# Eight 512-wide products of zeros among the transposes of the first query units

## The chip, the cores and the metric

The kernel runs on one core of one Trainium2 chip. The metric is the time of one execution on the device, in microseconds (us). Engines are named as in the profile: PE (TensorE, matrix products and transposes), PEld (its weight loads), DVE (VectorE), ACT (ScalarE), POOL (GpSimd), SP (SyncE, which issues most DMAs).

## What is computed

Agent attention, followed by a mixture of experts with one expert per token. There are 4 batches of 11456 tokens, 128 channels, 49 agents, 8 experts with 1024 hidden units. Cut to what matters:

```python
def sm(a, b):                                   # softmax of scaled scores
    s = scale * (a @ b.transpose(0, 2, 1))
    e = np.exp(s - s.max(-1, keepdims=True))
    return e / (e.sum(-1, keepdims=True) + 1e-09)
agent_v = sm(agents, k) @ v                     # per batch: 49 x 128
x = (sm(q, agents) @ agent_v).reshape(B * N, D)
logits = normed(x) @ normed(expert_emb).T / tau
idx, gate = argmax(logits), softmax(logits)[idx]
out[idx == e] = gate * (relu(x[idx == e] @ w1[e]) @ w2[e])
```

## The kernel before

A batch is cut into 12 units of up to 8 columns of 128 tokens. For each batch the keys come first (their scores against the agents, then the weighted sum of the values, `avp`), then the queries, then the feed-forward part with the one expert that nearly all tokens of the batch pick; the few other tokens are answered one by one. In batches 1 to 3 the keys of the next batch run beside the feed-forward part of the one before. Batch 0 has nothing to run beside, so its keys and the start of its queries stand alone, in `first()`.

The place of the change is the turn of batch 0 from keys to queries. When the values are summed, `av_chain` makes `avT` and the router's columns (`foldp`, `key`, `rp`), and the generator `pick_expert` starts: it has the expert's weights fetched (w1s, w2s, on SP's queue), multiplies them with `avT` (L606, tile `gp`), ranks the hidden units by a key (L645 spreads the key over a diagonal, L656 multiplies it with ones into `row`, L663 and L665 count on DVE and ACT how many are smaller), and sorts the units into place (`sel`, `placed`, then `gh` and `gl`). The first feed-forward product is `hp` (L1040, L1041). `linp` (L708), `w2pp` (L722) and `yp` come after it.

Meanwhile `q_unit` handles the queries. Units 0 and 1 of batch 0 are started first, units 2 and 3 after the first two have been turned; these four (LEAD is 4) run in a special form (`f32` is true). Each unit of 8 columns goes through these steps:

- `pe_T` turns the 8 columns with 8 fp32 transposes on PE into two PSUM banks (tile `fTp`, four columns a bank, from the pool of four banks `ps_h`). ACT copies the first bank out (L395), DVE the second (L393).
- Eight products with the agents give the scores (L773, `sp`). Each shows as two records in the profile.
- DVE takes the maximum and subtracts it (L777, L780), ACT takes the exponential (L782) and rounds it (L787), DVE makes the rest (L788).
- For the four first units, PE turns the result in f16 (L793, `tp`) and ACT copies it out (L794, `tt`). Other units use a DMA for this.
- 16 products with `r_hi` and `r_lo` (L809, L810, `rtp`) give the router's numbers.

`zeros` is a 128 x 512 f16 tile of zeros in SBUF. The kernel already multiplies it with itself 14 times at its start (`warm`, L170), in PSUM banks that nothing reads.

The order of instructions on each engine comes from a scheduler that works on priorities and on a simulated time line of its own: an instruction that is put in may move others. SP's order is fixed by hand (`manual_schedule`).

Of the kernel before, what the change touches and what calls it, by code (L numbers as in the profile page):

```python
# [18 lines left out]
P = 128  # L19
# [10 lines left out]
def kernel(ctx: ExitStack, tc: tile.TileContext, q, k, v, agents, emb, tau, w1, w2, out):  # L30
    nc = tc.nc
    pe, dve, act, pool, sp = nc.tensor, nc.vector, nc.scalar, nc.gpsimd, nc.sync
# [25 lines left out]
    GRP = 2  # L58
    LEAD = min(4, NU)
    LAG = 5  # L60
    HOLD = 2
    TB = 8
    XB = 3
# [20 lines left out]
    def pss(name):  # L84
        return ps_s.tile([P, 512], F32, name=name, tag="s")

    def psh(name):
        return ps_h.tile([P, 512], F32, name=name, tag="h")
# [11 lines left out]
    def take(o, uses=1):  # L100
        at = o.asked
        o.asked += 1
        while len(o.left) < at or (at >= o.n and o.left[at - o.n]):
            yield 1
        o.left.append(uses)
        return at

    def give(o, i):
        o.left[i] -= 1
# [8 lines left out]
    units, slot = {}, {}  # L118

    def used(*unit):  # L120

        ring[slot[unit]][1] = now[0]
# [9 lines left out]
    def unit_of(t):  # L132
        return (t // UT, t % UT) if t < NT - 1 else (NU - 1, 0)

    def ushape(u):
        return (P, min(UJ, J - u * UJ)) if u < NU - 1 else (REM_P, REM_J)

    def ucol(u):
        return min(u * UJ, J)
# [23 lines left out]
    zeros = cst.tile([P, 512], F16, name="zeros")  # L163
# [196 lines left out]
    def in_place(last):  # L360

        return tc.issue_after(last[-1].ins) if last else nullcontext()
# [17 lines left out]
        else:  # L380
            dve.tensor_tensor(out=mr, in0=spv, in1=mr, op=ALU.max)

    def pe_T(src, p, n):

        xT = wk.tile([P, 2 * UJ, P], F16, name="fT", tag="xT", bufs=XB).rearrange("k c p -> k (c p)").bitcast(F32)
        for c0 in range(0, n, TJ):
            m = min(TJ, n - c0)
            tp = psh("fTp")
            for c in range(m):
                pe.transpose(out=tp[:, c * p : (c + 1) * p], in_=src[:p, c0 + c, :], identity=ident[:p, :p])  # L390
            dst = xT[:, c0 * p : (c0 + m) * p]
            if c0:
                dve.tensor_copy(dst, tp[:, : m * p])  # L393
            else:
                act.copy(dst, tp[:, : m * p])  # L395
        return xT
# [362 lines left out]
    def q_unit(b, u, g):  # L759
        bt = batches[b]  # L760
        p, n = ushape(u)
        while ("q", b, u) not in units:
            yield 1
        tt_of[b, u] = yield from take(t_slots, n + sum(unit_of(t)[0] == u for t in range(NT)))
        f32 = b == 0 and u < LEAD
        i = yield from take(x_slots)
        with in_place(p_last):
            xT = pe_T(units["q", b, u], p, n)
        used("q", b, u)
        yield g[0]  # L770
        s = pss("sp")
        for c in range(n):
            pe.matmul(out=s[:p, c * A : (c + 1) * A], lhsT=xT[:, c * p : (c + 1) * p], rhs=aT_all[:, b, :], start=True, stop=True)  # L773
        give(x_slots, i)
        spv = s[:p, : n * A].rearrange("p (c a) -> p c a", a=A)
        mx = sm.tile([P, UJ], F32, name="qmx", tag="qmx")[:p, :n]
        dve.tensor_reduce(out=mx, in_=spv, axis=AX.X, op=ALU.max)  # L777
        ie = yield from take(qe_slots)
        e = wk.tile([P, UJ, A], F32, name="qe", tag="qe", bufs=LEAD)[:p, :n]
        dve.tensor_tensor(out=e, in0=spv, in1=mx.unsqueeze(2).broadcast_to([p, n, A]), op=ALU.subtract)  # L780
        yield g[1]
        act.activation(e, e, AF.Exp, scale=SCALE)  # L782
        yield g[2]
        i = yield from take(e_slots)
        e2 = e16[i % len(e16)]
        hi = e2[:p, :n, :A]
        act.copy(hi, e)  # L787
        (dve if f32 else pool).tensor_tensor(out=e2[:p, :n, LO : LO + A], in0=e, in1=hi, op=ALU.subtract)  # L788
        tt = wk.tile([P, UJ * P], F16, name="tt", tag="tt", bufs=TB)
        if f32:  # L790
            tp = psh("tp").bitcast(F16)
            for c in range(n):
                pe.transpose(out=tp[:, c * p : (c + 1) * p], in_=e2[:p, c, :], identity=ident16[:p, :p])  # L793
            act.copy(tt[:, : n * p], tp[:, : n * p])  # L794
        else:
            if ffn_at[0]:
                yield 4
            sp.dma_start_transpose(out=tt[:, : n * p].rearrange("k (c p) -> k c p", p=p),
                                   in_=e2[:p, :n, :].rearrange("p c k -> p (c k)"))
        give(e_slots, i)  # L800
        yield g[3]
        tts[b, u] = tt
        while not hasattr(bt, "r_hi"):
            yield 1
        s = (pss if ffn_at[0] else psh)("rtp")
        with in_place(y_last):
            for c in range(n):
                o = s[:p, c * RW : (c + 1) * RW]
                pe.matmul(out=o, lhsT=tt[:, c * p : (c + 1) * p], rhs=bt.r_hi, start=True, stop=False)  # L809
                pe.matmul(out=o, lhsT=tt[:, c * p : (c + 1) * p], rhs=bt.r_lo, start=False, stop=True)  # L810
        gi = group_of[u]
        us = groups[gi]
        if (b, gi) not in rtgs:
            rtgs[b, gi] = wk.tile([P, GC, E + 1], F32, name="rtg", tag="rtg", bufs=4)
        if not hasattr(bt, "qq"):
            bt.qq = sm.tile([P, 2, NCOL], F32, name="qq", tag="qq")
        rtg, qq = rtgs[b, gi], bt.qq
        c0 = ucol(u) - ucol(us[0])
        cs = slice(c0, c0 + n)
        if p < P:  # L820
            pool.memset(rtg[p:, cs], 1.0)
            pool.memset(qq[p:, :, ucol(u) : ucol(u) + n], 1.0)
        sv = s[:p, : n * RW].rearrange("p (c w) -> p c w", w=RW)
        rt = wk.tile([P, 2, UJ, A], F32, name="rt", tag="rt", bufs=1)[:p, :, :n]
        act.copy(rtg[:p, cs], sv[:, :, : E + 1])
        pool.tensor_tensor(out=rt[:, 1], in0=e, in1=e, op=ALU.mult)
        dve.tensor_tensor(out=rt[:, 0], in0=sv[:, :, E + 1 :], in1=e, op=ALU.mult)  # L827
        give(qe_slots, ie)
        yield 1
        pool.tensor_tensor(out=rt[:, :, :, : A // 2], in0=rt[:, :, :, : A // 2], in1=rt[:, :, :, A // 2 + 1 :], op=ALU.add)  # L830
        yield g[4]
        dve.tensor_reduce(out=qq[:p, :, ucol(u) : ucol(u) + n], in_=rt[:, :, :, : A // 2 + 1], axis=AX.X, op=ALU.add)
        routed[b, gi] = routed.get((b, gi), 0) + 1
        if routed[b, gi] == len(us):
            spawn(route_group(b, gi, sum(ushape(x)[1] for x in us)), 1, half=True)
# [74 lines left out]
    def proved(b, u, c):  # L910

        bt = batches[b]
        p, n = ushape(u)
        FV = FVS[b]
        at = slice(ucol(u) + c, ucol(u) + c + 1)
        z = psh("vp")
        with in_place(y_last):
            pe.matmul(out=z[:p, :FV], lhsT=tts[b, u][:, c * p : (c + 1) * p], rhs=bt.vm, start=True, stop=True)  # L918
        give(t_slots, tt_of[b, u])
        if c not in (0, 2, 4):  # L920
            act.activation(z[:p, :FV], z[:p, :FV], AF.Relu, bias=bt.l[:p, at], scale=-1.0, accum_out=bt.vsum[:p, at])  # L921
        else:
            dve.tensor_reduce(out=bt.vmin[:p, at], in_=z[:p, :FV], axis=AX.X, op=ALU.min)  # L923
        bt.seen += 1
# [3 lines left out]
    def prove():  # L928

        if jobs and ((jobs[0][0], HOLD) <= ffn_t[0] or jobs[0][0] == 0):  # L930
            proved(*jobs.pop(0))
# [355 lines left out]
    def spawn(g, at=0, half=False):  # L1287
        t0 = now[0] + (now[0] % 2)
        active.append([t0 + 2 * at, g, 1 if half else 2])
# [22 lines left out]
    def first():  # L1312
# [29 lines left out]
        for u in range(2):  # L1342
            spawn(q_unit(0, u, (1, 0, 0, 1, 0)))
# [6 lines left out]
        for u in range(2, LEAD):  # L1350
            spawn(q_unit(0, u, (1, 0, 0, 1, 0)))
# [67 lines left out]
    def queries():  # L1419
        start = now[0] // 2  # L1420
        for at, _, b, u in plan()[1]:
            while now[0] // 2 < start + at + 2:
                yield 1
            spawn(q_unit(b, u, (2, 1, 1, 5, 1)))
# [19 lines left out]
    with tc.manual_schedule(engines={mybir.EngineType.SP}):  # L1444
        due = []
        for i in range(len(ticks) + LAG):
            if i < len(ticks):
                b, t, r = ticks[i]
# [5 lines left out]
                if f is not None:  # L1454
                    with tc.high_priority(200):
                        ffn_mm1(b, t, f)
                    ffn_t[0] = (b, t)
                    due.append((i + LAG, b, t, f))
            else:
                run_half()  # L1460
            while due and due[0][0] <= i:
                _, b, t, f = due.pop(0)
# [49 lines left out]
```

## Time and profile before

| what | value |
|---|---|
| median of 3 runs | 800.28 us (799.91 to 804.07) |
| the profiled execution | 803.49 us |
| its span, first to last instruction | 801.7 us |
| mean granted clock of PE | 0.938 |
| PE busy | 729.7 us (91%) |
| PE weight loads | 614.5 us (77%) |
| DVE busy | 620.7 us (77%) |
| ACT busy | 487.2 us (61%) |
| POOL busy | 347.4 us (43%) |

A span is the time from the first to the last instruction of the profiled execution; its own time is 1.8 us longer. The granted clock is the share of its full clock at which PE was let run. Busy PE is not PE at its peak: its records overlap, and at half clock the same product takes twice as long.

### The profile page before, as it was taken

The numbers are of one execution on the slowest core, as the hardware profiler recorded it, in microseconds if no ns is written. First come the engines' busy times: TensorE is split into PE (matmuls) and PEld (weight loads), VectorE is DVE, ScalarE is ACT, GpSimd is POOL, SyncE is SP. The second block draws the span as 40 slices with busy tenths as digits, with TensorE's granted clock in tenths as the row PEclk, the third lists the DMA queues.
The fourth block names the chain that finished last, engine by engine and source line by source line (L and its number), as shares of the span: only waits on it lengthen the run. The fifth ranks groups of instructions, "written<-read, shape, count | busy, mean of one in ns | idle before, by whom it ended". The sixth has DMA issues, their size and how long they took to land.

```text
span 801.7 us, 21160 instructions
## 1 busy us (share of the span) xinstructions
PE 729.7 (91%) x8161; PEld 614.5 (77%) x8161; DVE 620.7 (77%) x1639; ACT 487.2 (61%) x1229; POOL 347.4 (43%) x602
## 2 busy tenths in 40 slices
PE   8979889989897979979999799999998898999995
PEld 6978678877786768768888588778886687877774
DVE  5554698887674999957678898966779987699876
ACT  2333475877664763657667944766579354666763
POOL 5000341445513743745433742685537445255520
PEclk9985589999997989989999999999999998999998
DMA  8766008997746946965596627986352235122311
GB/s 324 207 203 228 27 1 231 276 236 184 183 132 154 301 86 182 206 180 135 149 283 150 170 72 176 274 203 170 94 142 73 85 97 167 54 73 75 101 54 47
DMA packets 164050, 124.01 MB, mean 155 GB/s; under 512 B 84968, under 2 KB 140348, under 8 KB 163948
## 3 DMA queue, kind: packets, MB, share of 16 engines
q1 hardware_dynamic: 150571, 99.02, 47.5%
q10 hardware_dynamic: 13120, 23.47, 8.1%
q8 instruction: 65, 1.06, 0.5%
q14 instruction: 38, 0.30, 0.1%
q0 software_dynamic: 256, 0.15, 0.1%
HBM read 79.14 MB, written 23.72 MB: 128 GB/s over the span
## 4 chain that ended last, share of the span: by engine, by line
PE 58%; DVE 24%; DMA 8%; ACT 5%; issue 3%; POOL 1%; SPq 0%; ACTq 0%; POOLq 0%; DVEq 0%
PE sp L773 7%; PE fTp L390 6%; PE avp L487 5%; PE sp L411 5%; PE vp L918 4%; PE yp L1068 4%; PE yp L1070 4%; PE yp L1069 4%; PE hp L1040 3%; DVE hl L1045 3%; PE hp L1041 3%; PE yp L1059 3%; DMA tt<-e 3%; DMA kt<-in_k_dram 2%; DVE vmin L923 2%
## 5 line engine op out<-in xcount | busy, mean ns | idle before, releaser
L1045 DVE SCALAR_TENSOR_TENSOR hl<-hp,hh 128x512 f16<-128x512 f32 (+1 forms) x207 | 137.1, 666 | 31.8 <-ACT hh L1044 31.1
L1068 PE MATMUL yp<-w2p,hh 128*128 128x128 f16 (+1 forms) x810 | 157.9, 223 | 1.1 <-ACT hh L1044 0.6
L1069 PE MATMUL yp<-w2p,hh 128*128 128x128 f16 (+1 forms) x810 | 157.7, 222 | 0.0
L1070 PE MATMUL yp<-w2p,hl 128*128 128x128 f16 (+1 forms) x810 | 154.0, 222 | 3.4 <-DVE hl L1045 3.4
L921 ACT ACTIVATE vp<-vp,la 128x320 f32<-128x320 f32 (+1 forms) x224 | 121.7, 543 | 54.3 <-PE vp L918 42.1
L1044 ACT ACTIVATE hh<-hp 128x512 f16<-128x512 f32 (+1 forms) x207 | 120.6, 587 | 46.9 <-PE hp L1041 42.6
L918 PE MATMUL vp<-vm,tt 128*128 128x320 f16 (+1 forms) x360 | 109.5, 323 | 9.9 <-DVE hl L1045 4.3
L1068 PEld LDWEIGHTS <-hh 128*128 128x128 f16 (+1 forms) x810 | 81.8, 101 | 21.2 <-ACT hh L1044 5.1
L773 PEld LDWEIGHTS sp<-aT_all,fT 128*128 128x128 f32 x720 | 94.8, 207 | 3.1 <-DVE rt L827 0.3
L1070 PEld LDWEIGHTS <-hl 128*128 128x128 f16 (+1 forms) x810 | 81.2, 100 | 20.0 <-issue 6.6
L773 PE MATMUL sp<-aT_all,fT 128*128 128x49 f32 x720 | 96.1, 286 | 0.1
L1069 PEld LDWEIGHTS <-hh 128*128 128x128 f16 (+1 forms) x810 | 81.2, 100 | 8.0 <-issue 1.0
L923 DVE TENSOR_REDUCE vmin<-vp 128x1 f32<-128x320 f32 (+3 forms) x136 | 72.2, 531 | 17.6 <-PE vp L918 17.4
L1040 PE MATMUL hp<-tt,gh 128*128 128x512 f16 (+1 forms) x207 | 78.0, 380 | 6.6 <-ACT fT L395 2.1
L1041 PE MATMUL hp<-tt,gl 128*128 128x512 f16 (+1 forms) x207 | 78.0, 380 | 0.0
L788 POOL TENSOR_TENSOR e<-qe,e 128x392 f16<-128x392 f32 (+1 forms) x44 | 38.7, 880 | 81.6 <-ACT e L787 78.0
L869 POOL TENSOR_TENSOR nrm<-qq,half 128x16 f32<-128x16 f32 (+2 forms) x28 | 68.8, 2456 | 0.2
L395 ACT COPY fT<-fTp 128x512 f32<-128x512 f32 (+1 forms) x78 | 43.7, 563 | 38.6 <-PE fTp L390 29.9
L1083 DVE TENSOR_TENSOR ot<-yp,gs 128x512 f32<-128x512 f32 (+1 forms) x92 | 61.3, 668 | 7.4 <-PE yp L1070 7.2
L1059 PE MATMUL yp<-lin,tt 128*128 128x128 f16 x720 | 65.1, 221 | 1.7 <-DVE ot L1083 1.5
L390 PE MATMUL fTp<-ident,qt 128*128 128x128 f32 x360 | 60.6, 303 | 4.5 <-ACT vp L921 1.3
L393 DVE COPY fT<-fTp 128x512 f32<-128x512 f32 x70 | 47.8, 683 | 21.6 <-PE fTp L390 20.4
(358 smaller groups left out, 1750.4 us busy)
## 6 DMA issues: line engine op xcount, KB each, us to landing
kt<-in_k_dram SPq DMA_DIRECT2D x44, 512.0 KB, 6.4
vt<-in_v_dram SPq DMA_DIRECT2D x44, 512.0 KB, 5.3
qt<-in_q_dram SPq DMA_DIRECT2D x44, 512.0 KB, 5.1
out_dram<-ot ACTq DMA_DIRECT2D x88, 256.0 KB, 2.8
w1s<-in_moe_w_dram SPq DMA_DIRECT2D x8, 512.0 KB, 3.7
w2s<-in_moe_w_dram SPq DMA_DIRECT2D x8, 512.0 KB, 5.5
tt<-e SPq DMA_TRANSPOSE x44, 3.2
kt<-in_k_dram SPq DMA_DIRECT2D x4, 96.0 KB, 3.0
```

The costliest lines, as they stand in the source:

```text
L390: pe.transpose(out=tp[:, c * p : (c + 1) * p], in_=src[:p, c0 + c, :], identity=ident[:p, :p])
L773: pe.matmul(out=s[:p, c * A : (c + 1) * A], lhsT=xT[:, c * p : (c + 1) * p], rhs=aT_all[:, b, :], start=True, stop=True)
L918: pe.matmul(out=z[:p, :FV], lhsT=tts[b, u][:, c * p : (c + 1) * p], rhs=bt.vm, start=True, stop=True)
L921: act.activation(z[:p, :FV], z[:p, :FV], AF.Relu, bias=bt.l[:p, at], scale=-1.0, accum_out=bt.vsum[:p, at])
L1040: pe.matmul(out=hp[:, :m], lhsT=bt.gh[:, fs], rhs=tt, start=True, stop=False)
L1041: pe.matmul(out=hp[:, :m], lhsT=bt.gl[:, fs], rhs=tt, start=False, stop=True)
L1044: h_last[:] = [act.activation(hh[:, :m], hp[:, :m], AF.Relu)]
L1045: dve.scalar_tensor_tensor(out=hl[:, :m], in0=hp[:, :m], scalar=0.0, in1=hh[:, :m], op0=ALU.max, op1=ALU.subtract)
L1059: pe.matmul(out=yp[:p, c, :], lhsT=tc_, rhs=bt.lin[:, h], start=(c == 0 and h == 0), stop=False, skip_group_check=True)
L1068: pe.matmul(out=y, lhsT=hh[:, cs], rhs=wh, start=False, stop=False, skip_group_check=True)
L1069: pe.matmul(out=y, lhsT=hh[:, cs], rhs=wl, start=False, stop=False, skip_group_check=True)
L1070: y_last[:] = [pe.matmul(out=y, lhsT=hl[:, cs], rhs=wh, start=False, stop=last, skip_group_check=True)]
```

## The change

`pe_T` takes a number of fillers, and `q_unit` passes 1 for the four first units of batch 0 and 0 for all others. Each filler is one product of `zeros` with itself, 512 columns wide in f16, written into the bank that the next four transposes write. The transposes overwrite it, and nothing reads it. Two banks a unit and four units make eight fillers. The keys' calls of `pe_T` keep 0.

```diff
+    FILL = 1
...
-    def pe_T(src, p, n):
+    def pe_T(src, p, n, fill=0):
...
             tp = psh("fTp")
+            for _ in range(fill):
+                pe.matmul(out=tp, lhsT=zeros[:, :P], rhs=zeros, start=True, stop=True)
             for c in range(m):
                 pe.transpose(out=tp[:, c * p : (c + 1) * p], in_=src[:p, c0 + c, :], identity=ident[:p, :p])
...
-            xT = pe_T(units["q", b, u], p, n)
+            xT = pe_T(units["q", b, u], p, n, FILL if f32 else 0)
```

The lines of the changed kernel are one higher from L59 on, and three higher behind the loop of fillers (L390 becomes L393, L773 becomes L776).

PE, units 0 and 1, from the router's products to the products with the expert's weights. Before (tile names as in the steps above; qt are the loaded queries):

```order
L534 MATMUL rp<-avT 128x49
L390 MATMUL fTp<-ident,qt 128x128 x16
L238 MATMUL total<-avsq,ones 128x1
L773 MATMUL sp<-aT_all,fT 128x49 x12
L553 MATMUL avsT<-ident,avT 49x128
L773 MATMUL sp<-aT_all,fT 128x49 x4
L198 MATMUL mT<-ident,amx 1x128
L203 MATMUL mB<-ident,mTx 128x1
L606 MATMUL gp<-avT,w1s 128x49 x8
```

And now:

```order
L391 MATMUL fTp<-zeros 128x512
L393 MATMUL fTp<-ident,qt 128x128 x4
L391 LDWEIGHTS zeros
L391 MATMUL fTp<-zeros 128x512
L393 MATMUL fTp<-ident,qt 128x128 x4
L239 MATMUL total<-avsq,ones 128x1
L776 MATMUL sp<-aT_all,fT 128x49 x13
L556 MATMUL avsT<-ident,avT 49x128
L776 MATMUL sp<-aT_all,fT 128x49 x3
L199 MATMUL mT<-ident,amx 1x128
L204 MATMUL mB<-ident,mTx 128x1
L609 MATMUL gp<-avT,w1s 128x49 x8
```

Each four transposes have a filler ahead of them (the first two groups stand right ahead of these rows in the same form); the rest keeps its place but for one product of sp.

PE, units 2 and 3, behind the router's products of units 0 and 1. Before:

```order
L390 MATMUL fTp<-ident,qt 128x128 x12
L773 MATMUL sp<-aT_all,fT 128x49 x4
L390 MATMUL fTp<-ident,qt 128x128 x4
L773 MATMUL sp<-aT_all,fT 128x49 x12
L656 MATMUL row<-sel,ones 128x512 x2
```

And now, from the second of four groups on:

```order
L391 LDWEIGHTS zeros
L391 MATMUL fTp<-zeros 128x512
L393 MATMUL fTp<-ident,qt 128x128 x4
L391 LDWEIGHTS zeros
L391 MATMUL fTp<-zeros 128x512
L393 MATMUL fTp<-ident,qt 128x128 x4
L391 LDWEIGHTS zeros
L391 MATMUL fTp<-zeros 128x512
L393 MATMUL fTp<-ident,qt 128x128 x4
L776 MATMUL sp<-aT_all,fT 128x49 x16
L659 MATMUL row<-sel,ones 128x512 x2
```

All sixteen transposes now stand ahead of all sixteen products of sp.

ACT, behind the copies of row, where the rank is counted (sel,more) and the turned scores of units 2 and 3 are copied out (tt) and their router's numbers (rtg). Before:

```order
L665 ACTIVATE sel,more<-sel,nkey 128x1024
L787 CAST e_1_160<-qe 128x8x49
L883 ACTIVATE ex<-lga 128x64
L665 ACTIVATE sel,more<-sel,nkey 128x1024
L794 COPY tt<-tp 128x1024
L665 ACTIVATE sel,more<-sel,nkey 128x1024
L794 COPY tt<-tp 128x1024
L395 COPY fT<-fTp 128x512
L665 ACTIVATE sel,more<-sel,nkey 128x1024
L825 COPY rtg<-rtp 128x72 x2
L683 CAST gh<-placed 128x256
```

And now:

```order
L668 ACTIVATE sel,more<-sel,nkey 128x1024
L790 CAST e_1_160<-qe 128x8x49
L797 COPY tt<-tp 128x1024
L668 ACTIVATE sel,more<-sel,nkey 128x1024
L828 COPY rtg<-rtp 128x72
L668 ACTIVATE sel,more<-sel,nkey 128x1024
L797 COPY tt<-tp 128x1024
L668 ACTIVATE sel,more<-sel,nkey 128x1024
L398 COPY fT<-fTp 128x512
L828 COPY rtg<-rtp 128x72
L686 CAST gh<-placed 128x256
```

The copy of the second unit's scores comes two counts behind the first one's, where one count stood between them; PE's transposes tp and products rtp of these two units are taken apart in the same way. SP issues the same list in the same order as before. Further on, the instructions of PE, DVE, ACT and POOL are the same ones, in an order that differs at several hundred places.

## The prediction

> **What bounds the kernel now.** I read the page's slices first, then the chain of work that ended last in the stretch of the change, then busy time with the granted clock by stretches, and last single groups on PE.
>
> ```profile
> PE   8979889989897979979999799999998898999995
> PEclk9985589999997989989999999999999998999998
> ```
>
> A slice is 20 us. PE is 80% busy or more nearly everywhere, and the granted clock is full except in one long hole, slices 4 and 5 (60 to 100 us). There batch 0 turns from its keys to its queries: units 0 and 1, then 2 and 3, are turned (fTp), scored (sp), and the expert's columns are ranked (gp, row, sel).
>
> ```profile
> 62.26 3.44 PE fTp L390 x16
> 65.91 5.20 PE sp L773 x24
> ...
> 71.32 1.59 PE sp L773 x8
> ...
> 74.39 3.58 PE gp L606 x16
> ...
> 82.98 2.71 PE fTp L390 x12
> 85.68 1.57 PE sp L773 x8
> 87.26 0.88 PE fTp L390 x4
> 88.14 4.99 PE sp L773 x24
> 93.12 3.56 PE row L656 x4
> 96.71 0.58 ACT sel L657
> ...
> 104.39 1.15 ACT sel L665 x2
> ...
> 112.78 0.38 PE hp L1040
> 113.38 0.82 PE sp L411 x8
> ```
>
> These are start, length and work of the chain: up to 96.7 us the path is nearly all PE, and from there to the second feed-forward tile (hp, 112.78) it is mostly ACT and DVE. So a faster PE pays ahead of 96.7 and hardly between 96.7 and 112.8.
>
> ```profile
> 60.42:104.80 44.38, 39.19 (x232) 35.27 (x233) 26.26 (x76) 21.50 (x43) 8.64 (x16) 0.50 0.31 112
> 67.25:70.66 3.41, 3.41 (x18) 3.41 (x18) 1.40 (x3) 1.45 (x3) 0.00 (x0) 0.50 1.11 356
> 84.32:87.73 3.41, 3.41 (x18) 3.19 (x18) 2.96 (x10) 0.78 (x2) 2.67 (x7) 0.50 0.50 148
> 91.14:94.56 3.42, 3.42 (x12) 2.58 (x12) 1.40 (x3) 0.00 (x0) 0.00 (x0) 0.50 0.01 2
> 101.38:104.80 3.42, 3.42 (x43) 3.36 (x42) 3.11 (x8) 3.42 (x6) 0.14 (x1) 0.50 0.00 0
> ```
>
> Columns: stretch, length, busy us of PE, weight loads, DVE, ACT, POOL, then the clock. The clock is 0.50 for 44.38 us although PE is busy for 39.19 of them, and it comes back at 104.80. 44.38 is 13 times 3.41, so I cut the time into stretches of 3.41 us from 60.42. Busy time doesn't bring the clock back: three of the four short rows are 100% busy and the clock stays. What they differ in is how much of it *streams columns*. A transpose takes 3.44/16 = 0.215 us for 128 columns (1.68 ns a column). An sp record takes 5.20/24 = 0.217 us for 49 columns, worth 0.082 us: 38%, the rest is its weight load. So 67.25 to 70.66 (sp alone) streams 38%; 84.32 to 87.73 (about 9 transposes, 8 sp) streams (1.94 + 0.66)/3.41 = 76%; 91.14 to 94.56 (8 sp, then row from 93.1) some 65%. The stretch after which it rose held this:
>
> ```profile
> 101.66 1.91 PE L390 MATMUL fTp<-ident,qt 128*128 128x128 f32 x8
> 103.36 0.26 PE L809 MATMUL rtp<-r_hi,tt 128*128 128x58 f16 x1
> ...
> 104.84 0.19 PE L810 MATMUL rtp<-r_lo,tt 128*128 128x58 f16 x1
> ```
>
> Eight transposes and 32 rtp products (first and last shown) fill it from edge to edge with streaming, some 99%. A later rise, at 258.4 us, followed this stretch:
>
> ```profile
> L390 PE MATMUL fTp<-ident,qt 128*128 128x128 f32 x6 | 1.6, 409 | 0.1
> L1040 PE MATMUL hp<-tt,gh 128*128 128x512 f16 x2 | 1.3, 634 | 0.0
> L1041 PE MATMUL hp<-tt,gl 128*128 128x512 f16 x2 | 1.2, 623 | 0.0
> ```
>
> Six transposes and four 512-wide f16 products: (6 x 0.215 + 4 x 0.427)/3.41 = 88% (0.427 is worked out below). So the point lies between 76% and 88% of a stretch, and a mix of transposes and 512-wide products, just what the change makes, passes it.
>
> **The change part by part.** It adds 8 products of zeros on PE, one ahead of each four transposes in units 0 to 3 of batch 0, and removes nothing.
>
> ```profile
> 1.48 2.31 PE L170 MATMUL warm<-zeros 128*128 128x512 f16 x5 [1.48 <-POOL zeros L164]
> 5.17 1.03 PE L170 MATMUL warm<-zeros 128*128 128x512 f16 x2
> 113.00 0.38 PE L1041 MATMUL hp<-tt,gl 128*128 128x512 f16 x1
> ```
>
> *Price of a filler.* The same product, with the clock not yet up: (2.31 - 1.03)/3 = 0.427 us each. At full clock 512 columns take about 113.00 - 112.78 = 0.22 us, from hp to hp. The weight load stands beside the product ahead. Each unit's fillers write a bank that its transposes take anyway, so no new wait for a bank arises; DMA and SP issue the same list in the same order.
>
> *Units 0 and 1.* Four fillers at 0.427 = +1.7 us on the path. They stretch 3.44 us of transposes to 5.15 us of pure streaming, from 62.3 to 67.4. However the 3.41 us grid lies, one stretch holds 2.6 us or more of it plus sp or rp beside it: 83% at worst. With the grid of this execution 63.83 to 67.25 is full and the clock rises at 67.25. Then sp: 5.20 + 1.59 = 6.79 us becomes 32 x 0.103 = 3.3 (0.103 from the row at 113.38, 0.82/8): -3.5. Its cover is gone with it: next is gp, which needs the weights w1s.
>
> ```profile
> 69.05 1.06 ACT L607 ACTIVATE sel<-w1s 128x1024 f16<-128x1024 f32 x1 [1.47 <-DMA w1s<-in_moe_w_dram]
> 88.78 1.21 DVE L645 TENSOR_TENSOR sel<-ident,key 128x1024 f32<-128x1024 f32 x1
> ```
>
> They are there at 69.05, ahead of gp's new start at 72.6 (74.39 - 1.8), so no wait appears. Does gp gain too? If the clock holds, 3.58 becomes 16 x 0.103 = 1.65 and the small products around it lose 0.4: another -2.3. A clock that was lost again shows the limit:
>
> ```profile
> L918 PE MATMUL vp<-vm,tt 128*128 128x512 f16 x2 | 0.8, 392 | 0.0
> L1040 PE MATMUL hp<-tt,gh 128*128 128x512 f16 x1 | 0.4, 379 | 0.0
> L1041 PE MATMUL hp<-tt,gl 128*128 128x512 f16 x1 | 0.4, 379 | 0.0
> L1121 PE MATMUL sqT<-ident,xq 128*128 128x128 f32 x1 | 0.3, 301 | 2.5 <-DMA xq<-in_q_dram,ix 2.5
> ```
>
> This is the stretch 671.40 to 674.82, after which it fell: four 512-wide and a few narrow products, at full clock's 0.22 us per 512 columns some 1.06 us of 3.41, 31%. The stretch with gp has 38% at most while gp runs, and gaps around mT and mB; I take it that the clock falls, gain 0. Units 0 and 1: +1.7 - 3.5 = -1.8 (bounds +1.7 if nothing rises, -4.1 if it holds).
>
> *Units 2 and 3.* Again four fillers, +1.7, and 5.15 us of streaming right behind rtp. The order also puts all 16 sp products behind all 16 transposes, where 4 of them stood in between; the same work, but one unbroken block. The clock rises in it or at its end. Then sp 1.57 + 4.99 = 6.56 becomes 3.3 (-3.3) and row 3.56 becomes 1.8 (-1.8). Next late is DVE's diag, ended at 89.99 and row at 93.12: 3.1 us of slack, of which 1.7 - 3.3 takes 1.6, so it doesn't bind. Sum -3.4 (bounds: +1.7, and -5.5 where transposes run fast too and DVE binds).
>
> *Behind 96.7.* ACT and DVE set the pace and carry the shift on at its length. The moved order splits tp and rtp of units 2 and 3 (second rtp half behind two more of ACT's sel passes), so the 99% stretch that ended the hole is broken up, and the clock may come later than before, relative to hp. Nearest rows: sp and placed there; each stretch at half clock costs 1.7 us at most, all under ACT or DVE to 0. I take 0, between 0 and 5 (three stretches). From hp on, the stages run in their own order with all engines above half busy, so an earlier start should reach the end. There the same instructions stand in another order at several hundred places on all engines but SP; I find no sign for it, and give it plus or minus 3 us.
>
> *The sum.* -1.8 - 3.4 = -5.2 on a traced execution that took 803.49 us (span 801.7): 798.3. But the median of the runs shown is 800.28 (799.91 to 804.07), 3.2 below it. I read part of that as the grid lying elsewhere: where a stretch falls within 0.4 us of the 3.44 us of transposes (0.8 of 3.41 positions, a quarter) or on rtp and the transposes at 82 us, the kernel before rises by itself, and the change gains only 1.5 or so. With 0.7 and 0.3, an estimate, 0.7 x 5.2 + 0.3 x 1.5 = 4.1, and 800.28 - 4.1 = **796.2 us**.
>
> [...]
>
> **The rivals.**
> (a) *The fillers don't lift the clock*, since transposes count for little. Then fillers stream 1.7 of 5.15 us, 33%, below all that rose; 8 x 0.427 = 3.4 us stay on the path: 803.7. Against it: the two rises above. 6 in 100.
> (b) *Slower: the end of the hole moves out.* The broken 99% stretch leaves the clock at half from row through placed, hp, the key transposes and linp. It decides from 2.4 stretches on (4.1/1.7) in which PE alone is the path; four to six of them make 800.28 - 4.1 + 6.8 = 803 to 806.4. For it: in the old order that one stretch alone passed. Against it: placed and hp are 256 and 512 wide and stream fully. 12 in 100.
> (c) *Half of it is lost*: only one pair of units lifts the clock in time, or the shift is eaten in the moved order behind 112.8: 797 to 802. 30 in 100.
> (d) *The clock holds through gp and row*: -4.1 - 5.5 = -9.6 at most, 790 to 792. 10 in 100.
>
> **How the numbers follow.** My forecast has 42 in 100, with its own range 793 to 798. I take 0.5% (4 us) as what a measurement tells from none: faster is below 796.3. From the forecast a good 35 and from (d) 10, with little of (c), make 0.47 faster; (a), most of (c) and the rest of the forecast 0.39 the same; (b) and a bad draw of the moved order 0.14 slower. The range leaves out the ends of (b) and the best of (d): 790.5 to 803.
>
> **What would show it.** Granted clock 1.00 from about 67 us for one stretch, again from about 82 to 86; sp records 0.10 us apart there; row at 1.8 us; gp still at 0.22 a record; the second hp some 5 us earlier than 112.78; the same shift at the end. It is wrong if the clock stays 0.50 through both blocks, if row comes earlier and hp doesn't, or if hp comes earlier and the end doesn't.

## The result, and the profile after

The changed kernel takes 805.51 us (median of 20 runs, 798.07 to 815.10), the kernel before, run beside it, 800.24 us (20 runs, 792.62 to 807.61). The ratio is 1.0083, 95% interval 1.0054 to 1.0113: slower by 5.3 us, where 796.2 was predicted. Medians here and below are of all runs, while the ratios leave out executions more than 1.5% above the quickest of their kernel. The profiled execution took 806.97 us (span 805.2, mean granted clock 0.950; before: 803.49, 801.7, 0.938).

So the clock is higher and the kernel slower. The slices of the page, 20 us each, PE's busy tenths and its clock:

```profile
PE   8977799989897969989999889899999799999995
PEclk9987799999997996999999999999999999999998
```

The hole of slices 4 and 5 (5, 5 before) is now 7, 7. In its place slice 16 (300 to 320 us) has clock 6, where it had 9. PE is busy for less of slices 4 and 5 (7, 7 for 9, 8), since the same work takes it less time there (the 64 records of sp 7.5 us for 14.1, row 1.9 for 3.7). By stretches (columns as in the prediction):

```profile
49.21:69.69 20.48, 16.24 (x216) 15.41 (x213) 10.59 (x35) 5.91 (x13) 0.11 (x1) 1.00 1.00 358
69.69:83.34 13.65, 10.11 (x76) 9.01 (x77) 8.76 (x30) 9.45 (x21) 2.17 (x4) 0.50 0.13 50
83.34:93.58 10.24, 7.74 (x59) 6.09 (x57) 9.81 (x23) 4.26 (x10) 6.92 (x10) 1.00 0.16 52
93.58:100.41 6.83, 5.18 (x53) 4.59 (x54) 6.83 (x15) 6.55 (x14) 3.53 (x9) 0.50 0.01 2
301.80:315.45 13.65, 12.38 (x61) 10.89 (x62) 8.71 (x29) 2.52 (x5) 2.49 (x6) 0.50 0.05 12
```

The 44.38 us at half clock became 13.65 and 6.83. The fifth row is 13.65 us at half clock while PE is 91% busy. The kernel before ran at full clock from 299.36 to 315.45 us; its own fall there comes earlier and is half as long:

```profile
292.53:299.35 6.82, 4.84 (x35) 4.39 (x35) 6.82 (x32) 1.72 (x6) 1.89 (x11) 0.50 0.92 148
```

The head did gain, and by more than the forecast's 5.2. The copy that ends the expert's sorting (tile gh), in before and after (duration in ns, then first and last start):

```profile
L683 ACT CAST gh<-placed x1: 372/372/372, 109.4 to 109.4; 128x256 f16<-128x256 f32 x1
```

```profile
L686 ACT CAST gh<-placed x1: 373/373/373, 103.3 to 103.3; 128x256 f16<-128x256 f32 x1
```

It is 6.1 us earlier. Followed along the kernel by the copies of hp (tile hh, 207 of them), the lead is 6.8 us at 113, 2.6 at 175, 1.0 at 235 and 0 at 290 us. Part of this isn't the order: from 159 to 262 us no instruction stands elsewhere, yet the lead falls there from 5.7 to 1.2 us, with two falls of the clock for 3.41 us (at 168.68 and 216.46) that the profile before doesn't have. It then turns into a lag of 5 us at 327, next to none from 390 to 415, 7.5 from 560 to 625, 12 at 672, and 3.7 at the end. The turn of sign is at the hand-over from batch 0 to batch 1. There PE waits between 280 and 360 us for (us in total, times, longest):

```profile
PE rtp L812 <- DMA tt<-e: 4.4, 2, 3.2
PE linp L711 <- POOL gts L707: 2.3, 1, 2.3
PE hp L1043 <- DVE hl L1048: 1.6, 1, 1.6
```

These waits gave the places to test: linp behind gts, and rtp behind the DMA that turns the scores (tt).

### The profile page after: what moved, and what is told of

Same layout as the page of the kernel before. It is cut to its first block, busy times and chain, and to the rows that moved or that the text cites. A ratio compares the mean times of both kernels' runs of the same rounds, so it can differ in the third digit from the quotient of the medians.

```text
span 805.2 us, 21181 instructions
## 1 busy us (share of the span) xinstructions
PE 724.2 (90%) x8169; PEld 607.4 (75%) x8169; DVE 622.4 (77%) x1639; ACT 487.3 (61%) x1229; POOL 349.7 (43%) x602
## 4 chain that ended last, share of the span: by engine, by line
PE 56%; DVE 23%; DMA 10%; ACT 5%; issue 3%; POOL 1%; SPq 0%; ACTq 0%; DVEq 0%; POOLq 0%
PE sp L776 5%; PE avp L490 5%; PE fTp L393 5%; PE sp L414 5%; PE vp L921 5%; DMA kT<-ks 4%; PE yp L1071 4%; PE hp L1043 4%; PE yp L1072 4%; PE yp L1073 4%; PE hp L1044 3%; PE yp L1062 3%; DVE hl L1048 3%; DMA kt<-in_k_dram 2%; DVE sel L666 2%
## 5 line engine op out<-in xcount | busy, mean ns | idle before, releaser
L1071 PE MATMUL yp<-w2p,hh 128*128 128x128 f16 (+1 forms) x810 | 155.2, 220 | 0.7 <-DVE w2p L727 0.3
L1072 PE MATMUL yp<-w2p,hh 128*128 128x128 f16 (+1 forms) x810 | 155.0, 220 | 0.0
L1073 PE MATMUL yp<-w2p,hl 128*128 128x128 f16 (+1 forms) x810 | 151.8, 220 | 3.4 <-DVE hl L1048 3.4
L776 PEld LDWEIGHTS sp<-aT_all,fT 128*128 128x128 f32 x720 | 88.6, 195 | 4.6 <-ACT gh L686 1.2
L776 PE MATMUL sp<-aT_all,fT 128*128 128x49 f32 x720 | 89.8, 275 | 1.3 <-ACT gh L686 1.1
L1062 PEld LDWEIGHTS <-tt 128*128 128x128 f16 x720 | 50.6, 101 | 14.1 <-issue 8.2
```

The costliest lines, as they stand in the source:

```text
L1062: pe.matmul(out=yp[:p, c, :], lhsT=tc_, rhs=bt.lin[:, h], start=(c == 0 and h == 0), stop=False, skip_group_check=True)
L1071: pe.matmul(out=y, lhsT=hh[:, cs], rhs=wh, start=False, stop=False, skip_group_check=True)
L1072: pe.matmul(out=y, lhsT=hh[:, cs], rhs=wl, start=False, stop=False, skip_group_check=True)
L1073: y_last[:] = [pe.matmul(out=y, lhsT=hl[:, cs], rhs=wh, start=False, stop=last, skip_group_check=True)]
```

## The experiments

In the diff the eight products come with a new order of the same instructions at several hundred places. The first group of runs separates the two. For this each engine's order is written out as a table, and the instructions are bound to it without a wait (`pin_order`). All twelve runs are pinned so; in the profiles PE, DVE, ACT and POOL of e1 run exactly the sequence of the kernel before (fillers aside), and those of e2 that of the changed kernel. Their line numbers are 39 higher than the changed kernel's in most (L711 becomes L750), 36 higher in e2, 40 in e3 and e12. e1:

```diff
-                pe.matmul(out=tp, lhsT=zeros[:, :P], rhs=zeros, start=True, stop=True)
+                fillers.append(pe.matmul(out=tp, lhsT=zeros[:, :P], rhs=zeros, start=True, stop=True).ins)
...
+    pin_order(tc, fillers)  # PE, DVE, ACT, POOL in the order of the kernel before; a filler ahead of its transposes
```

> The changed kernel's eight fillers, but every engine's instructions pinned to the order of the kernel before; the fillers stand ahead of their transposes. Theory 1 (the moved order is what costs): the start of batch 0 gains its 6 us as in the changed kernel (first hp near 103 us) and keeps them, 793 to 796 us. Theory 2 (the gain of the start is given back later whatever the order, since the hand-overs between batches set the pace): first hp near 103 us as well, but the end at 799 to 806 us.

e2 is the reverse, the kernel before (no fillers) in the changed kernel's order:

```diff
+    pin_order(tc, fillers)  # an empty list; PE, DVE, ACT, POOL in the order of the changed kernel
```

> The kernel before without fillers, but every engine's instructions pinned to the order of the changed kernel. Theory 1: the start is as late as before or later (first hp at 109 to 112 us, clock at half through it) and the moved order adds its loss of some 10 us: 808 to 814 us. Theory 2: the order is neutral, 798 to 803 us.

Medians over all runs, us:

| | order of before | changed order |
|---|---|---|
| no fillers | 800.03 (29 runs; ratio 1) | e2: 806.25 (6 runs), ratio 1.0116 [1.0065, 1.0167] |
| eight fillers | e1: 792.49 (12 runs), ratio 0.9917 [0.9878, 0.9956] | the changed kernel: 805.51 |

In the old order the fillers gain 7.5 us; e1 beats both kernels, just under Theory 1's 793 to 796. The changed order costs 6 us without fillers and 13 with them, and in it they gain 0.7, which is no difference. e2 lies between its two forecasts (808 to 814 and 798 to 803), and the late start that Theory 1 gave it was wrong. e1's clock did what the prediction wrote down:

```profile
60.23:67.05 6.82, 6.43 (x26) 5.43 (x27) 1.86 (x8) 1.51 (x4) 0.00 (x0) 0.50 1.03 408
67.05:73.88 6.83, 6.00 (x54) 5.79 (x54) 5.39 (x21) 4.31 (x11) 0.84 (x1) 1.00 0.76 259
73.88:84.12 10.24, 9.22 (x74) 8.10 (x74) 6.93 (x24) 6.47 (x11) 3.10 (x7) 0.50 0.11 21
84.12:94.36 10.24, 6.65 (x54) 5.10 (x54) 8.75 (x18) 5.60 (x12) 4.58 (x9) 1.00 0.08 32
94.36:97.77 3.41, 3.32 (x42) 3.11 (x41) 3.01 (x8) 3.41 (x6) 0.12 (x1) 0.50 0.00 0
```

It rises at 67.05 and at 84.12, and for good at 97.77, where before had 104.80; gh comes at 102.4, 7.0 us earlier than before. In e2's profile gh is at 103.2, as early as in the changed kernel: there the clock rose at 83.06 with no filler, where the sixteen transposes of units 2 and 3 stand unbroken by sp, and at 60 us the clock hadn't fallen (it was full from 49.0 to 69.4). So in that execution the gain of the head didn't need the fillers.

**What lifts the clock.** e3 replaces each filler by two more fp32 transposes, e4 by one fp32 product 49 columns wide, e12 by two that are 16 wide; all in the order of before.

```diff
-                fillers.append(pe.matmul(out=tp, lhsT=zeros[:, :P], rhs=zeros, ...).ins)
+                for c in range(2):                                                    # e3
+                    fillers.append(pe.transpose(out=tp[:, c * P : (c + 1) * P], in_=ident, identity=ident).ins)
...
+                fillers.append(pe.matmul(out=tp[:, :49], lhsT=ident, rhs=ident[:, :49], ...).ins)   # e4
...
+                for c in range(2):                                                    # e12
+                    fillers.append(pe.matmul(out=tp[:, c * 16 : (c + 1) * 16], lhsT=ident, rhs=ident[:, :16], ...).ins)
```

> The order of the kernel before, and in place of each filler two more fp32 transposes of the identity into the same bank: about the same PE time (2 x 0.215 us), no zeros and no f16. If streamed columns of transposes count towards the clock as those of products do (my reading), the clock rises in both blocks as with the fillers and the time is that of the pinned kernel with fillers, within 3 us. [...]

> The order of the kernel before, and in place of each filler one fp32 product of 49 columns with the identity (two records of 0.217 us, the same PE time as a filler, but 38% of it streams columns, the rest loads weights). If streamed columns count (my reading), the clock stays at half unless a stretch of 3.41 us happens to fall on the 16 transposes, first hp 2 to 3 us later than before, 802 to 805 us. If busy time of PE counted, the clock would rise as with the fillers, 793 to 797 us.

> In the order of before, each of the eight products of zeros is replaced by two fp32 products 16 columns wide with the identity: by the sp records (0.217 us each at half clock, two a product, whatever their width) they keep PE busy for twice as long as one filler, 0.87 us instead of 0.427, but stream only an eighth of it. If the clock goes by streamed columns (a stretch of transposes and these would stream some 55%): no rise at about 67 us or at 84 us, and the time is the old order's without fillers plus up to 3.5 us a pair of units, 800 to 807. If the clock goes by busy time: it rises at both places, and the time is 792.5 and up to 5 us more, 793 to 797.5.

e3: 791.72 us (10 runs; 0.9917 [0.9879, 0.9956]). The stretch after which its clock rose, at 68.12, is nothing but transposes (PE's groups in it; busy us, mean ns, idle time before):

```profile
L433 PE MATMUL fTp<-ident,qt 128*128 128x128 f32 x12 | 3.3, 412 | 0.0
L431 PE MATMUL fTp<-ident 128*128 128x128 f32 x6 | 1.9, 421 | 0.0
```

e4: 793.96 us (10 runs, 786.95 to 801.95; 0.9916 [0.9867, 0.9965]), and the clock rose at 67.36 and 84.43. I had expected no rise: a miss, since those stretches, with four transposes to each narrow product, still streamed some 81% and 74%, an estimate by the prediction's way of counting. It told nothing apart. e12 does: 804.92 us (10 runs; 1.0044 [1.0007, 1.0081]), 12 us over e1. Its profiled execution took 811.78 us, and I read the clock alone from it:

```profile
61.61:65.02 3.41, 3.41 (x17) 3.41 (x18) 0.86 (x5) 0.22 (x2) 0.00 (x0) 0.50 1.03 410
65.02:68.43 3.41, 3.41 (x19) 3.41 (x19) 0.69 (x1) 0.80 (x2) 0.00 (x0) 0.50 0.94 379
...
88.91:92.33 3.42, 3.42 (x18) 3.42 (x19) 1.99 (x7) 0.81 (x2) 1.39 (x4) 0.50 0.26 51
```

PE is 100% busy in all three, streams 36 to 63% by the same estimate, and the clock stays at 0.50, in one piece from 61.61 to 102.57. The narrow records were shorter than the 0.217 us expected "whatever their width": 8 transposes of 0.215 us and 11 of them fill 65.02 to 68.43, which leaves an estimated 0.15 us for each. So busy time alone didn't lift the clock here, and streamed columns, as estimated, fit these stretches. Of the stretches counted, it rose behind those of 81% and more (e4, e3, the two of the prediction) and not behind those of 63% and less (e12). In between the estimate doesn't tell: it rose behind e4's of 74%, and stayed behind before's of 76% and of 78% (80.90 to 84.32: 24 rtp products 0.048 us apart and 1.53 us of transposes).

**Where the moved order costs.** Mixed orders, all with the eight fillers, take one order up to a point and the other behind it, or one order inside a window alone. e5 is e1 with some 170 instructions around the hand-over from batch 0 to 1 as in the changed kernel; e6 is the changed kernel with that same place as before. What e5 moves on DVE, ACT and POOL, cut to the main rows:

```diff
 DVE
+L869 TENSOR_TENSOR rt<-rtp,qe 128x392
 L736 TENSOR_TENSOR mask<-mask,key 128x8
...
+L727 CAST gl<-placed 128x256
...
+L1125 TENSOR_TENSOR ot<-yp,gs 96x256
...
+L874 TENSOR_REDUCE qq<-rt 128x2x8
 L741 TENSOR_SCALAR mask<-rank 128x8
+L1087 SCALAR_TENSOR_TENSOR hl<-hp,hh 128x512
 L743 SCALAR_TENSOR_TENSOR mask<-sgn,mask 128x8
...
 POOL
+L872 TENSOR_TENSOR rt<-rt 128x16x24
+L868 TENSOR_TENSOR rt<-qe 128x392
 L746 TENSOR_TENSOR gts<-gts,mask 128x8x49
...
 ACT
 L725 CAST gh<-placed 128x256
+L1086 ACTIVATE hh<-hp 128x512
+L478 ACTIVATE ks<-kt,hsc 128x8x128
...
 L753 ACTIVATE lin<-linp 128x128
```

> The eight products, the order of before everywhere, but for some 200 instructions (PE 102, VectorE 45, ScalarE 14, GpSimd 8) around the hand-over from the first batch to the second (about 290 to 300 us), which stand as in the changed kernel: on VectorE the four steps that make the mask of gts stand behind a square sum and a 512-wide hl of the turn, on GpSimd gts stands behind two rt steps, on ScalarE a hh and a ks stand ahead of lin. In the changed kernel linp began 8.0 us after gh, with the old order 2.6 us after it, and the clock fell for 13.65 us behind that gap. Theory A (the moved order costs most of its time at this one place): 5 to 10 us more than the old order with the products (792.5), so 797 to 803, linp 6 us or more behind gh, and the clock at half speed for two stretches or more behind it. Theory B (the cost is made of many small places along the kernel): no more than 2 us of it here, 791 to 795.

> The changed kernel's order everywhere, with the eight products, but for the same place around the hand-over from the first batch to the second, which stands as before. Theory A: 5 to 10 us less than the changed kernel (805.5), so 795 to 801, with linp within 4 us of gh and no fall of the clock there. Theory B: 803 to 806, since the other places keep their cost.

e5: 798.28 us (12 runs), 5.8 more than e1. e6: 800.14 us (12 runs), 5.4 less than the changed kernel. The ratios to the kernel before are 1.0053 [1.0005, 1.0101] and 1.0072 [1.0022, 1.0122]. e5 to e8 ran on another chip than the other experiments; the kernel before has a median of 801.25 us on it (35 runs, 789.07 to 811.73), against 800.03 beside e1. Resampling the runs gives a difference of two medians a 95% interval of some 3 to 5 us either way (e5 over e1: 3.0 to 9.2; e6 under the changed kernel: 0.9 to 9.0). Some 170 of about 5000 moved positions make some 40% of the order's cost (5.4 or 5.8 of 13.0). The chain there, first in the changed kernel:

```profile
298.84 0.47 DVE qq L835
...
299.55 0.10 DVE hl L1048
299.65 0.43 issue
300.08 0.20 DVE mask L704
...
300.37 0.88 POOL gts L707
...
301.31 1.72 POOL gts L707
...
303.07 3.78 PE linp L711 x16
306.85 3.28 PE sp L776 x16
```

and in e1:

```profile
294.27 0.07 DVE mask L743
294.35 0.09 DVE rank L774
294.44 0.87 POOL gts L746
...
295.53 0.92 POOL gts L746
...
296.50 2.05 PE linp L750 x16
298.55 1.72 PE sp L815 x16
```

The last step of the mask that gts waits for takes 0.2 us on DVE. In e1 it ends 0.4 us after gh (293.9); in the changed kernel five steps that e1 has behind it stand ahead of it (rt, gl, a 256-wide ot, a turn's sum qq and a 512-wide hl), and it ends 5.2 us after gh (295.1). The five don't all cost by their length. DVE is busy without a gap there in the changed kernel, but in e5, where the mask ends 5.2 us after gh too, half of that is a wait of gl for PE, and the mask stands behind gl:

```profile
DVE gl L727 <- PE placed L720: 2.5, 1, 2.5
```

In the changed kernel PE runs dry until linp (busy for 3.06 of the 7.40 us from 295.50 to 302.90), the clock falls at 301.80, and then linp and sp take 7.06 us at half clock, which took 3.77 in e1. In e5's trace the copies of hp run level with e1's up to 285 us (0.4 us ahead) and are some 6.3 us late from 335 to 640 us. Its gap from gh to linp is 7.1 us (e1: 2.6, changed kernel: 8.0), and its clock was low for 3.41 us behind it, not for the two stretches that I had expected:

```profile
PE vp L960 <- DVE hl L1087: 2.8, 1, 2.8
PE hp L1082 <- DVE hl L1087: 1.8, 1, 1.8
PE linp L750 <- POOL gts L746: 1.4, 1, 1.4
```

Those are PE's waits in e5 from 285 to 306 us. The first stands in e1 too (2.9), the second is new, and the third is 0.7 in e1. linp comes 4.2 us later than in e1; the low stretch behind it is what is nearest for the rest of the 6.3, which no run takes apart.

The rest was looked for with e7 (changed order up to about 235 us, then the old one; what it moves lies between 68 and 155 us), e8 (old order up to about 320 us, then the changed one), e9 (e1 with a second small place, 325 to 350 us, as in the changed kernel), e10 (the changed kernel with both small places as before) and e11 (old order up to about 425 us, then the changed one).

> The eight products; the changed kernel's order up to about 235 us, the order of before behind it. In the profiles the changed kernel had lost 3 us to the old order with the products by 235 us, and 19 us at the end. Theory A: 792 to 795 (the hand-over stands in the old order). Theory B (many places): some 3 us of it are in this part, 795 to 798. A theory that the head's order is what costs, and the rest follows from it: 803 to 806.

> The eight products; the order of before up to about 320 us, with the first hand-over, and the changed kernel's order behind it. In the profiles the changed kernel lost 9 of its 19 us to the old order with the products behind 320 us, 7 of them by 421 us. Theory A: 792 to 795. Theory B: 798 to 803.

> The eight products and the order of before, but for a second small place (about 325 to 350 us: PE 123 instructions, VectorE 25, ScalarE 19, GpSimd 14), which stands as in the changed kernel: on ScalarE three kd steps stand ahead of the rounding of the scores (e, CAST), which the DMA that turns them (tt) waits for, and the products rtp of that tt stand on PE ahead of hp and yp. In the run with the changed order behind 320 us, PE waited 4.1 us there for tt, and the clock was low for 6.83 us. Theory A2 (a few such places, where a queue's order puts the work that PE needs next behind a turn's other steps, make the whole cost): a PE wait for tt of 3 us or more, the clock low behind it, and 2 to 5 us over the old order with the products (792.5): 794.5 to 797.5. Theory B (the cost is spread thinly over the several hundred moved places): no more than 1 us: 792 to 793.5.

> The changed kernel's order with the eight products, but for the two small places (hand-over of batch 0 to 1, and the wait for tt at about 340 us), which stand as before. The hand-over alone gave 800.1. Theory A2: another 2 to 4 us back, 796 to 798, with no PE wait for tt of 2 us or more at 330 to 350 us. Theory B: 799 to 801, as with the hand-over alone.

> The eight products; the order of before up to about 425 us, the changed order behind it (the hand-over from batch 1 to 2 too, where linp began 10.5 us after gh in the changed kernel and 5.8 with the old order). Behind 320 us as a whole the changed order cost 4.9 us (797.4). Theory A2: this hand-over is one of the places, 2 to 4 us: 794.5 to 796.5. If the rest behind 425 us costs nothing: 791.5 to 793.5, and all of the 4.9 lies between 320 and 425 us.

| run | changed order where | median, us | over e1 (792.49) |
|---|---|---|---|
| e7 | up to 235 us | 796.08 (12 runs) | +3.6 |
| e5 | hand-over, about 290 to 300 us | 798.28 (12 runs) | +5.8 |
| e9 | about 325 to 350 us | 794.08 (6 runs) | +1.6 |
| e8 | behind 320 us | 797.39 (12 runs) | +4.9 |
| e11 | behind 425 us | 793.43 (6 runs) | +0.9 |
| e10 | all but the two small places | 795.95 (12 runs) | +3.5 |
| changed kernel | all | 805.51 (20 runs) | +13.0 |

Up to 235 us, hand-over and behind 320 us add up to 14.3, the whole is 13.0. Putting the hand-over back gives 5.4, and the second place another 4.2 (e6 to e10). With such intervals e9's 1.6 and e11's 0.9 can't be told from nothing, and neither, by a little, can e10's 4.2 (-0.7 to 7.4). Neither theory holds alone. The hand-over is one place that costs 6; of the rest, 3.6 lie ahead of 235 us (95% interval 0.4 to 8.2), which Theory B alone had expected; e8's 797.4 falls between the two forecasts; and behind 425 us there is next to nothing. The ratios to before: e7 1.0004 [0.9956, 1.0052], e8 1.0038 [0.9987, 1.009], e9 0.9898 [0.9852, 0.9945], e10 0.9943 [0.9909, 0.9976], e11 0.9888 [0.9839, 0.9938].

At the second place my expectation was wrong in the mechanism, and e9's time lies just under its range (794.08 for 794.5 to 797.5). PE's wait for tt, in e9 and then in e1:

```profile
PE rtp L851 <- DMA tt<-e: 3.1, 1, 3.1
```

```profile
PE rtp L851 <- DMA tt<-e: 1.9, 2, 1.1
```

The longest such wait grew by 2.0 us, and the clock fell for 6.83 us behind it. But the rounding of the scores that this tt waits for ran before the kd steps, not behind them. The DMA itself was longer: 11.9 us from its issue to its landing, against 9.6 in e1. In the five runs with the changed order at this place (the changed kernel, e2, e6, e8, e9) it took 11.0 to 12.2 us. With the old order it took 9.6 or 9.7 in e1, e4, e5, e7, e10 and e11, but 10.3 in e3, 11.1 in e12 and 11.9 in the kernel before. So in these traces the long transfer goes with the changed order, but not with it alone; what else decides it is left open.

Of the 3.6 us ahead of 235, one place shows in the traces. In the changed order ACT's first pass over the expert's weights (sel, L610) stands ahead of its step r_hi (L548). That pass waits for the DMA of w1s, so r_hi waits too, then DVE behind r_hi, then PE. In the changed kernel, from 58 to 75 us:

```profile
ACT sel L610 <- DMA w1s<-in_moe_w_dram: 5.6, 1, 5.6
DVE r_lo L549 <- ACT r_hi L548: 5.6, 1, 5.6
PE mT L199 <- DVE r_lo L549: 4.1, 1, 4.1
```

In all five runs with this order in the head (the changed kernel, e2, e6, e7, e10) PE waits for 0.8 to 5.1 us ahead of mT, in the nine with the old order not at all (in e5 and e8 it waits 3.0 and 2.4 us for the same pass, but a product later, at mB). It costs most where the clock is full up to about 70 us: there gp begins at 73.2 to 73.8 us with the changed order (the changed kernel, e2, e10) and at 70.8 with the old one (e5, e8). By gh 0.8 to 1.8 us of that are left. e7's wait was 0.8 us, so this place doesn't make all of its 3.6; the others are left open.

## Why the prediction was wrong, and where it was right

- *Units 0 and 1*: right in the old order up to gp. The clock rose at 67.05 (67.25 forecast), and gp began 2.1 us earlier than before (72.2 for 74.3; forecast 1.8). But it held until 73.88, into gp, whose 16 records took 2.16 us for 3.65: another 1.5 us where the forecast took "gain 0". In the changed kernel the size came near by luck. Its clock didn't even fall at 60 us and held from 49.21 to 69.69, as it did without fillers in e2; gp at 73.22 gained only 1.2, at half clock as forecast, since PE stood idle for 4.1 us behind the weights (rows above). "So no wait appears" was wrong there, and in e5 and e8 too, where the clock held as long.

```profile
73.22 3.60 PE gp L609 x16
```

- *Units 2 and 3*: right in the old order. The clock rose at 84.12 (forecast: between 82 and 86; changed kernel: 83.34). From the end of gp to the end of row e1 gained 3.5 us, and 3.4 were forecast (changed kernel: 5.0; its clock rose 1.8 us into the block of transposes, e1's 4.9). The whole shift at row's end, forecast as 5.2, was 7.1 us in e1 (89.6 for 96.7) with gp's 1.5, and 6.2 in the changed kernel (90.5).
- *The end of the hole*, rival (b): it didn't move out. The clock was back at 100.41 for the rest of the head (before: 104.80), and gh kept the gain. That the measured time is close to (b)'s 803 to 806.4 is luck: it has another cause.
- *The median's share*: 4.1 us were forecast, by a guess of how often before lifts its clock by itself because the grid lies elsewhere. No run shows that term: in the one traced execution of before the clock stayed at half from 60.42 to 104.80, and the traces show only that the grid lies elsewhere in each (last section). e1 measured 7.5, by its interval 3.5 to 9.8, which has the 4.1 in it.
- *The moved order*: the step that failed. Of the instructions that stand "in another order at several hundred places", the prediction says "I find no sign for it, and give it plus or minus 3 us". It cost 13 us with the fillers and 6 without, and that turned the head's gain into a loss. The sign was there to be looked for. The order of the changed kernel has DVE's last mask step and POOL's gts behind a turn's steps at the hand-over, and the chain of before runs there on PE alone, from placed to linp, with nothing to spare. In the head it has ACT's r_hi behind the pass that waits for w1s. The chain of before at the hand-over:

```profile
300.44 0.96 PE placed L678 x8
301.40 0.43 PE hp L1040 x2
301.83 1.97 PE linp L708 x16
```

- *Rival (a)*: refuted. The clock rose behind a stretch of fp32 transposes alone (e3, from 0.50 to 1.00 at 68.12 us).
- The test that the prediction named ("if hp comes earlier and the end doesn't") is what came true.

## What to carry to other kernels

When a scheduler sets the order, a change of a few instructions is two changes; pin the old order and measure both, since here the one gained 7.5 us and the other lost 13. In a moved order, read first the places where a chain of short steps on other engines feeds PE, and look there for a step that waits itself: five steps of a turn, one of them waiting for PE, set ahead of a 0.2 us mask on DVE cost 6 us, a part of it through the clock, and a pass that waits for a DMA, set ahead of r_hi on ACT, kept PE idle for 4.1. To judge whether the clock rises behind a stretch, estimate its streamed columns: here the clock rose behind those of 81% and more and stayed behind those of 63% and less, while PE's busy time told nothing (100% in e12, and the clock stayed at 0.50).

## What the hardware showed beside that

In the traces of before and of the changed kernel every length at one clock, from the first fall to the last, is a multiple of 3.41 us, from 3.41 to 174.08. The grid that these changes make lies elsewhere in each of these runs: the first fall is at 43.36 us in before and at 42.38 in the changed kernel, and the fall near 60 us is at 60.42 in before, 60.23 in e1 and 61.61 in e12. And the same work lost the clock in one run and kept it in another. e8 has the same instructions in the same order as e1 up to 313 us. In e1 the clock fell at 60.23 (row above); in e8 it held:

```profile
49.84:70.33 20.49, 16.20 (x215) 15.27 (x211) 13.24 (x42) 7.35 (x18) 0.10 (x1) 1.00 1.01 361
```

The last grid stretch ahead of that point, in e1 and then in e8, is nearly the same:

```profile
56.81:60.23 3.42, 1.91 (x28) 1.54 (x24) 1.72 (x6) 0.00 (x1) 0.00 (x0) 1.00 1.01 411
```

```profile
56.67:60.08 3.41, 1.98 (x29) 1.61 (x24) 1.65 (x6) 0.07 (x1) 0.00 (x0) 1.00 1.01 396
```

e8's has one record of PE more (29 for 28), since its grid lies 0.06 us earlier against the work (foldp begins 1.89 us into the stretch, 1.83 in e1). So this place stands at the edge, if it is the grid that decides; no run shows that it is.

Each of these profiles has 9 to 13 stretches at half clock, and the runs of one kernel spread over up to 23 us (35 runs of the kernel before), so that it takes some 10 runs to see 5 us, an estimate from the intervals above. How much of the spread comes from the grid no run tells.
